# Attention and a capacity-limited mixture of experts on Trainium2: counting keys over fixed levels instead of a stepwise search, with the value logits split over four tiles and constants loaded later

## The chip, the cores and the metric

The kernel runs on one core of one Trainium2 chip. The metric is the device time of one execution in microseconds (us); a profiled execution also gives a span, from its first to its last instruction, which is a little shorter. TensorE (PE) does the matmuls, VectorE (DVE), ScalarE (ACT) and GpSimd (POOL) the element-wise work, and SyncE (SP) issues most of the transfers. Each engine works through its own instructions in order and waits for the others by semaphores.

## What is computed

```python
# q, k, v: 8 batches x 8 heads x 576 rows x 64, cut into chunks of 64 rows
scores = scale * q_c @ k_c^T                  # within a chunk, scale = 1/8
attn = exp(scores - max); attn /= attn.sum(-1) + 1e-9
x = (attn @ v_c), rows of all heads side by side     # N = 4608 rows x D = 512

logits = x @ w_gate                           # 8 experts
expert_idx = argmax(logits, axis=1)
gate_w = softmax(logits)[expert_idx]
for e in range(8):
    tok_idx = rows with expert_idx == e
    keep the `capacity` (80) of them with the greatest gate_w
    out[tok_idx] = gate_w * (relu(x[tok_idx] @ w1[e]) @ w2[e])     # F = 1024
# all other rows of out are zero
```

Everything is float32. The gate weight of a row's own expert is called its key; the kernel looks for a threshold per expert that about 80 keys pass, and then ranks the few rows that are left.

## The kernel before

The 4608 rows are 36 tiles of 128 (RT). Tiles 0 to 31 hold the first 512 rows of each of 8 batches, four tiles a group; tiles 32 to 35 hold the last 64 rows of every batch. The order of the work is written out by hand: one loop over i (L838 to L881) runs a pipeline over the tiles, and every engine gets its instructions in the order of that code.

Iteration i does the scores of tile i (TensorE, s, L330), then their row maximum and subtraction on VectorE (mx L336, sm L339). If a group of four is complete, it does its gate matmul (L464) and a copy (L470). Then come the transposes of sm of tile i-1 (pt, L360) with ScalarE's exponential that empties them (pT, L362), the values of tile i-2 (o, L387 or L377) with VectorE's division (rc L397 and L398, x L415), the transposes of x of tile i-3 (px, L351) with ScalarE's copy (xT, L458), and at its end the loads of qk and v some tiles ahead (NB = 8 and NV = 7 buffers). pt and px take turns in one PSUM bank (tag "tp"), so each waits until ScalarE has emptied the other. Weights of the first experts and the clearing of the output are issued at iterations that the tables EARLY and CLEAR name.

Small steps on VectorE ride in the gaps: `fill()` (L286) is called five times a tile and takes one step from the queue of bounds, one from the queue of gates, and one more from that of bounds. A step may also issue a ScalarE or a TensorE instruction, which then stands in that engine's order at this place.

The keys of the first 16 tiles (NS) give an interval that holds each expert's threshold. `search_keys` (L585) transposes them to kT, and three rounds narrow it by four each: `search_count` (ScalarE signs sg L625 with an accumulator, VectorE hits L629), `search_sum` (L632, one matmul) and `search_move` (L637, some VectorE steps, the last of which, nt and th, are read by the next round's signs). `bounds` (L677) makes an interval of 254 levels per expert. For each tile, `levels` (L542) turns the keys into a level number bo, and 256 signs (ScalarE `signs` L557) or steps (GpSimd `steps_` L562) of it are counted by `tally` (L567): matmuls with `mine`, the rows' expert as one of eight columns, and 256 levels as two halves of 128, plus a row of ones for tiles that hold signs; `left_add` (L697) subtracts each group's counts on VectorE. LEVELS says behind which tile each step of this is queued.

The tiles 32 to 35 get their gate logits another way: the values' own logits (v times w_gate, head by head) stand in the last 8 of 73 columns of vh, the values of those tiles. `value_logits` (L442) makes them in iteration 30, as 64 matmul calls (two instructions each) in one piece, from vT, which is loaded in two halves into buffers of qk; ScalarE copies them (L452).

Behind the loop stand the last tile's work, the tallies of tiles 28 to 35, `threshold` (L715), a mask, ranks, and the row numbers of each expert's kept rows; matmuls without use (`keep_warm`, L751) fill TensorE's pauses there. Then `experts` gathers the rows from the scratch copy xs (L179), and runs both layers (L204, L237) for six groups of 128 slots.

Of the kernel before, what the change touches and what calls it, by code (L numbers as in the profile page):

```python
# [8 lines left out]
F32 = mybir.dt.float32  # L9
BF16 = mybir.dt.bfloat16  # L10
# [11 lines left out]
NB = 8  # L22
NV = 7
# [8 lines left out]
NBP = NS // 2 * 8  # L32
NIT = 3
# [4 lines left out]
LEVELS = {15: "l0:4 c0 c1 c2 - - - - s2 c3", 19: "l4:5 - s3 s0 c4", 23: "l5:6 s4 s1 c5",  # L38
          27: "l6:7 s5 c6 - - - - - s6"}
LV, LP = 7, 8  # L40
# [4 lines left out]
EARLY = {6: [0], 14: [1], 22: [2], 28: [3, 4], 29: [5], 30: [6], 31: [7]}  # L45
CLEAR = {32: [0], 33: [1], 34: [2, 3]}


C_ID, C_IO, C_TR, C_TAU, C_BLK = 0, 128, 384, 512, 640
C_A = C_BLK + NBP  # L50
# [5 lines left out]
C_J3 = C_J + 48  # L56
C_F3 = C_J3 + 3
C_D3 = C_F3 + 3
C_V3 = C_D3 + 3
NCONST = C_V3 + 3  # L60


@with_exitstack
def attention_moe(ctx: ExitStack, tc: tile.TileContext, qk, vv, v8, vt, wg, w1, w2, cap, cst, out):
# [23 lines left out]
    step = cp.tile([P, NE], F32, name="step")  # L88
    thr = cp.tile([P, NE], F32, name="thr")
    idp = cp.tile([P, P], BF16, name="idp")  # L90
    rst = cp.tile([P, NE, RT], BF16, name="rst")
    low = cp.tile([P, NE], F32, name="low")
    slot_oob = cp.tile([P, NR], F32, name="slot_oob")
    inw = cp.tile([P, NE], F32, name="inw")
    left = cp.tile([P, 2, NE], F32, name="left")
    lob = cp.tile([P, NE], F32, name="lob")
# [172 lines left out]
    with ExitStack() as actx:  # L269
# [3 lines left out]
        ps2 = actx.enter_context(tc.tile_pool(name="ps2", bufs=2, space=PSUM))  # L273
# [3 lines left out]
        S = {}  # L277
        gates, bounds_q = deque(), deque()

        def step_one(queue):  # L280
            if queue:
                fn, args = queue.popleft()
                fn(*args)

        def fill():

            step_one(bounds_q)
            step_one(gates)
            step_one(bounds_q)

        def flush(queue):
            while queue:
                step_one(queue)
# [7 lines left out]

        vh = wk.tile([P, 4, 8, VX], F32, name="vh", tag="vh", bufs=1)
# [52 lines left out]
        def probs(i):  # L355
# [7 lines left out]
            d['pT'] = pT  # L363

        def values(i, last=False):
# [26 lines left out]
            d['pov'] = po[:, :, 0:260].rearrange("p j (m x) -> p j m x", m=4)  # L392

# [48 lines left out]
        def value_logits():  # L442

            pv = ps2.tile([P, 4, 8, NE], F32, name="pv", tag="g")
            for r in range(4):
                for c in range(8):
                    for h in range(2):
                        o = 64 * h
                        nc.tensor.matmul(pv[o:o + 64, r, c, :],
# [768 lines left out]
```

## Time and profile before

| what | us |
|---|---|
| median of three runs (264.30, 264.91, 267.28) | 264.91 |
| the profiled execution's own time | 263.62 |
| its span | 261.8 |
| first expert layer starts | 160.42 |
| last expert layer ends | 254.81 |
| TensorE busy, of the span | 237.4 (91%) |
| VectorE, ScalarE, GpSimd busy | 130.5, 76.1, 53.2 |
| mean granted clock of TensorE | 0.962 |

A row of the timeline reads: start, duration, engine, line, operation, result <- operands, shape, count, and in brackets how long the engine had been idle and who released it. A row of the windows reads: the stretch and its length, then for each engine busy time and number of instructions, the granted clock, the mean share of the DMA engines and GB/s. A row of the groups reads: line, engine, operation, shape, count, busy us, mean ns of one, and the idle time just before them. A row of the waits reads: who waited for whom, us in all, times, the longest. TensorE's float32 matmuls are two instructions each; a loading of weights (PEld) stands beside the matmul it belongs to.

### The profile page before, as it was taken

What the parts mean: (1) busy time and instruction counts of PE and PEld (TensorE: products, weight loads), DVE (VectorE), ACT (ScalarE), POOL (GpSimd) and SP (SyncE); (2) the same over time, 40 slices, a digit from 0 to 9 for tenths busy, and PEclk for the clock granted to TensorE, in tenths of its full rate; (3) what the DMA queues carried; (4) which work ended last, traced back from release to release, by engine and by line L of the source; (5) the groups of instructions that cost most, each with busy time, mean ns of one, the idle gap of its engine ahead of it and who ended that gap; (6) DMA issues with size and microseconds to landing.
All of it is one profiled execution on the core that took longest, in us unless ns stands there. A gap on an engine that the chain in (4) does not pass through costs nothing. (4 is left out here: it accounts for less than half of the span.)

```text
span 261.8 us, 8338 instructions
## 1 busy us (share of the span) xinstructions
PE 237.4 (91%) x3584; PEld 141.4 (54%) x3584; DVE 130.5 (50%) x423; ACT 76.1 (29%) x157; POOL 53.2 (20%) x115
## 2 busy tenths in 40 slices
PE   8789999999998798899888898999999999999970
PEld 5677767676766666868756573342423324232310
DVE  6688696968797779325869854111211211121210
ACT  2125434344454436325744400120200102010000
POOL 6021030303030304920312836100000111010110
PEclk9999999999999999859999799999999999999995
DMA  7999999999999999999997305999999999995011
GB/s 246 304 358 368 406 397 404 353 374 390 408 356 409 413 412 377 348 412 400 405 401 301 100 0 155 382 387 408 396 401 408 402 398 395 405 386 196 3 38 36
DMA packets 32554, 86.01 MB, mean 328 GB/s; under 512 B 3264, under 2 KB 3392, under 8 KB 32384
## 3 DMA queue, kind: packets, MB, share of 16 engines
q1 hardware_dynamic: 28768, 72.50, 72.9%
q0 software_dynamic: 3456, 12.32, 12.5%
q10 hardware_dynamic: 288, 0.59, 0.9%
q8 instruction: 30, 0.49, 0.8%
q14 instruction: 12, 0.10, 0.1%
HBM read 65.22 MB, written 20.45 MB: 327 GB/s over the span
## 5 line engine op out<-in xcount | busy, mean ns | idle before, releaser
L204 PE MATMUL hc<-w,xtc 128*32 128x512 f32 x384 | 44.2, 594 | 0.2 <-ACT xtc L194 0.2
L237 PE MATMUL yc<-w,htc 128*32 128x512 f32 x384 | 43.3, 593 | 0.0
L387 PE MATMUL o<-vb,pT 128*64 128x130 f32 x512 | 36.2, 283 | 0.2 <-PE pt L360 0.2
L336 DVE TENSOR_REDUCE mx<-s 128x8 f32<-128x512 f32 x36 | 24.7, 685 | 15.7 <-PE s L330 15.2
L387 PEld LDWEIGHTS o<-vb,pT 128*64 128x64 f32 x512 | 28.4, 138 | 5.7 <-issue 5.1
L362 ACT ACTIVATE pT<-pt 128x512 f32<-128x512 f32 x36 | 21.5, 597 | 23.8 <-PE pt L360 23.4
L237 PEld LDWEIGHTS yc<-w,htc 128*32 128x32 f32 x384 | 12.5, 110 | 29.1 <-issue 28.2
L330 PE MATMUL s<-qk 64*64 64x64 f32 x1152 | 25.8, 227 | 2.3 <-issue 1.6
L360 PE MATMUL pt<-ct,sm 128*128 128x128 f32 x144 | 24.0, 290 | 3.8 <-ACT xT L458 2.7
L204 PEld LDWEIGHTS hc<-w,xtc 128*32 128x32 f32 x384 | 12.1, 110 | 26.0 <-issue 25.6
L339 DVE TENSOR_TENSOR sm<-s,mx 128x512 f32<-128x512 f32 x36 | 24.9, 691 | 0.7
L415 DVE TENSOR_TENSOR x<-o,rc 128x512 f32<-128x512 f32 x36 | 24.8, 689 | 0.5
L458 ACT COPY xT<-px 128x512 f32<-128x512 f32 x32 | 18.6, 580 | 19.6 <-PE px L351 19.4
L330 PEld LDWEIGHTS s<-qk 64*64 64x64 f32 x1152 | 20.9, 136 | 5.3 <-issue 2.6
L360 PEld LDWEIGHTS pt<-ct,sm 128*128 128x128 f32 x144 | 15.4, 143 | 14.6 <-issue 7.5
L243 POOL DMA_INDIRECT out<-ysc,si x6 | 6.0, 995 | 84.7 <-DMA out<-zero 42.3
L209 ACT ACTIVATE hsc<-hc 128x512 f32<-128x512 f32 x6 | 3.6, 598 | 64.3 <-PE hc L204 64.3
L428 POOL DMA_DIRECT2D xs<-x x8 | 6.6, 820 | 75.5 <-DVE keys L509 69.5
L242 DVE TENSOR_SCALAR ysc<-yc,gatec 128x512 f32<-128x512 f32 x6 | 4.5, 751 | 34.4 <-PE yc L237 34.4
L351 PE MATMUL px<-ct,x 64*128 64x64 f32 x256 | 14.8, 235 | 1.4 <-ACT pT L362 1.4
L211 DVE TENSOR_SCALAR hsc<-hc 128x512 f32<-128x512 f32 x6 | 4.1, 691 | 22.6 <-PE hc L204 22.6
L226 DVE COPY htc<-hpc 128x512 f32<-128x512 f32 x6 | 4.1, 692 | 22.0 <-PE hpc L222 22.0
(163 smaller groups left out, 264.3 us busy)
## 6 DMA issues: line engine op xcount, KB each, us to landing
w<-in_w SPq DMA_DIRECT2D x12, 2048.0 KB, 20.3
qk<-in_qk SPq DMA_DIRECT2D x35, 512.0 KB, 7.3
out<-zero SPq DMA_DIRECT2D x9, 1024.0 KB, 13.8
vb<-in_vv SPq DMA_DIRECT2D x64, 130.0 KB, 6.8
xs<-x POOLq DMA_DIRECT2D x8, 1024.0 KB, 9.9
w<-in_w SPq DMA_DIRECT2D x8, 1024.0 KB, 10.3
vh<-in_v SPq DMA_DIRECT2D x1, 1168.0 KB, 11.0
vT<-in_vt SPq DMA_DIRECT2D x2, 512.0 KB, 8.3
```

Of the source, the lines that this page charges most:

```text
L204: nc.tensor.matmul(h[o:o + 32, :], lhsT=xT[r][:, b, o:o + 32], rhs=getw(groups[r][g])[0][:, b, 512 * f:512 * f + 512], start=(b == 0), sto ...
L237: nc.tensor.matmul(y[o:o + 32, :], lhsT=hT[r][c // 4][:, c % 4, o:o + 32], rhs=getw(groups[r][g])[1][:, c, :], start=(c == 0), stop=(c == ...
L330: nc.tensor.matmul(ps[64 * u:64 * u + 64, h, 64 * pr:64 * pr + 64], lhsT=t['q'][64 * h:64 * h + 64, pr, u, :], rhs=t['k'][64 * h:64 * h + ...
L336: nc.vector.tensor_reduce(mx, s8, axis=AX.X, op=ALU.max)
L339: nc.vector.tensor_tensor(sm.rearrange("p c h k -> p h c k" if T == 8 else "p c k h -> p h c k"), s8, mx[:, :, :, None].to_broadcast([P, 2 ...
L351: nc.tensor.transpose(pm[:, u, 64 * pr:64 * pr + 64], src(pr)[rows], ident[rows, rows])
L360: nc.tensor.transpose(pt[:, pr, :], sv[:, pr, :], ident)
L362: nc.scalar.activation(pT, pt, AF.Exp, scale=0.125)
L387: nc.tensor.matmul(po[64 * u:64 * u + 64, pr // 2, o:o + 130].rearrange("p (h x) -> p h x", h=2), lhsT=d['pT'][:, pr, 64 * u:64 * u + 64], ...
L415: nc.vector.tensor_tensor(t['x'][:, r, :].rearrange("p (m j e) -> p j m e" if T == 8 else "p (j m e) -> p j m e", j=2, m=4), U[i]['pov'][. ...
L428: nc.gpsimd.dma_start(xs[T * 576:T * 576 + 512].rearrange("(c p) d -> p c d", p=P), t['x'])
L458: nc.scalar.copy(t['xT'][:, :, P * r:P * r + P].rearrange("p a (u j) -> p a u j", u=2), pm)
```

## The change

The search is replaced by counts over 128 fixed levels. For each of the first 16 tiles, `hist_sign` (ScalarE, L630 of the changed kernel) compares 128 fixed levels (and one that all pass) with the rows' keys, 128x129, and `hist_add` (TensorE, L638) adds them up by expert, in PSUM (tile ph, 8 rows x 129). `bounds` reads from the counts the interval for each expert on 8 partitions, with two VectorE instructions that multiply by the levels' distances and accumulate, and some small ones.

The counts of the levels are kept by expert too: `tally` is one matmul of 129 columns per tile into one PSUM tile pc, without `left_add`; there are 126 levels where 254 were, and signs are 128x129, steps 128x128. For this PSUM bank the pool ps2 has two tags with one buffer each in place of one tag with two.

ScalarE's small work (the exponentials of the gates and all signs) goes through two queues, `exps` and `signs_q`. An entry may be taken four fills after it was queued (LAG), by `act_slot`: at most two behind the exponential pT, at most one behind the copy xT. TensorE's counts go through a queue `counts`, at most four at an iteration's end (`pe_slot`), an iteration after their sign. `drain` empties all queues behind the loop.

`value_logits` does 16 calls (32 instructions) behind the values of each of the tiles 28 to 31, into free columns of their PSUM bank, and ScalarE copies them behind the next xT. vT has a buffer of its own, loaded at iteration 22, and vh is loaded at 25; NB is 7, NV 6. Three loads of constants move behind the loads of tile 5, and a fourth (hc, the fixed levels) is new; `late_constants` comes one iteration later. EARLY and CLEAR change a little.

On TensorE, before, where the value logits stand as one piece (tile 30's scores are behind, s_2295 is tile 31's):

```order
L351 MATMUL px_2218<-ct,x_1872 128x64 x8
L449 MATMUL pv<-wgp,vT_1751 64x8 x32
L449 MATMUL pv<-wgp,vT_1752 64x8 x32
L330 MATMUL s_2295<-qk_1840 64x64 x16
L464 MATMUL L_2320<-xT_1873,wgp 32x512 x4
L360 MATMUL pt_2327<-ct,sm_2170 128x128 x4
L387 MATMUL o_2334<-vb_105,pT_2177 64x130 x8
```

The changed kernel at the same place, from the scores of tile 30 to those of tile 31:

```order
L356 MATMUL s_2137<-qk_1827 64x64 x16
L386 MATMUL pt_2168<-ct,sm_2089 128x128 x4
L414 MATMUL o_2181<-vb_111,pT_2096 64x130 x8
L476 MATMUL o_2181<-wgp,vT 64x8 x16
L377 MATMUL px_2212<-ct,x_1871 128x64 x8
L624 LDWEIGHTS mine
L624 MATMUL pc<-lv_2099,mine 8x129
L624 LDWEIGHTS mine
L624 MATMUL pc<-lv_2128,mine 8x129
L356 MATMUL s_2230<-qk_1902 64x64 x16
```

A quarter of the value logits now stands between the values and px, and three more such pieces follow in the next iterations; the counts by expert (pc) stand at the iteration's end.

On ScalarE, before, at the first round of the search, between two exponentials pT:

```order
L592 COPY kT<-pk 64x256
L362 ACTIVATE pT_1558<-pt_1553 128x512
L625 ACTIVATE sg_0_1577,cn_1576<-kT,nt 64x256
L625 ACTIVATE sg_1_1579,cn_1576<-kT,nt 64x256
L458 COPY xT_1284<-px_1584 128x4x128
L470 COPY lt_1625<-L_1620 128x512
L362 ACTIVATE pT_1632<-pt_1627 128x512
```

ScalarE in the changed kernel, at the first group's signs (hv, of tiles 0 to 3, in iterations 11 and 12):

```order
L490 COPY xT_499<-px_777 128x4x128
L630 ACTIVATE hv_787<-hc,gg_590 128x129
L504 COPY lt_819<-L_814 128x512
L388 ACTIVATE pT_826<-pt_821 128x512
L630 ACTIVATE hv_828<-hc,gg_590 128x129
L630 ACTIVATE hv_830<-hc,gg_590 128x129
L490 COPY xT_763<-px_858 128x4x128
L630 ACTIVATE hv_868<-hc,gg_590 128x129
L388 ACTIVATE pT_904<-pt_899 128x512
```

The signs stand in the same places, behind a pT or an xT, but they read constants and the keys (gg) of a group that was gated before, not a step of the same search; they stand in iterations 11 to 24, and there are sixteen of them where the search had six.

On VectorE, before, in the search's first move (jk, jx, lo and wd are its steps):

```order
L397 TENSOR_SCALAR rc_1643<-o_1634 128x8
L398 RECIPROCAL rc_1643<-rc_1643 128x8
L645 SCALAR_TENSOR_TENSOR jk_1648,n_1649<-pc_1645,cv 64x3
L650 SCALAR_TENSOR_TENSOR jx_1651,lo<-jk_1648,ct 64x3
L415 TENSOR_TENSOR x_1560<-o_1634,rc_1643 128x512
L650 SCALAR_TENSOR_TENSOR jx_1654,wd<-jk_1648,ct 64x3
L656 TENSOR_SCALAR lo<-lo 64x1
L336 TENSOR_REDUCE mx_1701<-s_1684 128x8
```

VectorE in the changed kernel, where the interval is read from the counts ph:

```order
L362 TENSOR_REDUCE mx_1781<-s_1764 128x8
L583 TENSOR_TENSOR mine<-wt_1679,mw_1682 128x32
L660 TENSOR_SCALAR c_1576<-ph,cap_100 8x1
L365 TENSOR_TENSOR sm_1785<-s_1764,mx_1781 128x2x256
L662 TENSOR_SCALAR c_1576<-ph 8x1
L664 SCALAR_TENSOR_TENSOR n_1577,lo_101<-ph,c_1576,hc 8x128
L426 TENSOR_SCALAR rc_1806<-o_1797 128x8
L667 SCALAR_TENSOR_TENSOR n_1577,hi_102<-ph,c_1576,hc 8x128
```

What were many steps over 64 partitions is now two instructions over the 128 levels and a few small ones, once.

The diff, cut to its core:

```diff
-NB = 8
-NV = 7
+NB = 7
+NV = 6
...
-LEVELS = {15: "l0:4 c0 c1 c2 - - - - s2 c3", 19: "l4:5 - s3 s0 c4", 23: "l5:6 s4 s1 c5",
...
+LAG = 4
...
-        ps2 = actx.enter_context(tc.tile_pool(name="ps2", bufs=2, space=PSUM))
+        ps2 = actx.enter_context(tc.tile_pool(name="ps2", bufs=1, space=PSUM))
...
+        def act_slot(most):
+
+            for _ in range(most):
+                ready = [q for q in (exps, signs_q) if q and S['t'] - q[0][0] >= LAG]
+                if ready:
+                    ready[0].popleft()[1]()
+
+        def pe_slot(most=4):
+
+            for _ in range(most):
+                if not counts or counts[0][0] > S['i']:
+                    return
+                counts.popleft()[1]()
...
             nc.scalar.activation(pT, pt, AF.Exp, scale=0.125)
             d['pT'] = pT
+            act_slot(2)
...
             d['pov'] = po[:, :, 0:260].rearrange("p j (m x) -> p j m x", m=4)
+            if i >= 28:
+                value_logits(i - 28, po[:, 0, 320:384].rearrange("p (c e) -> p c e", c=8))
...
-            pv = ps2.tile([P, 4, 8, NE], F32, name="pv", tag="g")
-            for r in range(4):
-                for c in range(8):
-                    for h in range(2):
...
+            for c in range(8):
+                for h in range(2):
+                    o = 64 * h
+                    nc.tensor.matmul(pv[o:o + 64, c, :], lhsT=S['vT'][o:o + 64, r, c, :],
+                                     rhs=wgp[o:o + 64, c // 2, 0:NE], start=True, stop=True)
+            S['pv'] = r, pv
...
-            lv = gk.tile([P, 2 * P], BF16, name=f"lv{rt}", tag="lv", bufs=LV)
-            nc.scalar.activation(lv, io_b, AF.Sign, bias=bo[:, rt:rt + 1], scale=-1.0)
-            U[rt].update(lv=lv, signs=True)
+            lv = gk.tile([P, P + 1], BF16, name=f"lv{rt}", tag="lv", bufs=LV)
+            nc.scalar.activation(lv, io_l, AF.Sign, bias=bo[:, rt:rt + 1], scale=-1.0)
+            U[rt]['lv'] = lv
...
+            nc.tensor.matmul(S['pc'][:, 0:lv.shape[1]], lhsT=mine[:, rt, :], rhs=lv,
+                             start=S['cnt'] == 0, stop=last)
...
+        def hist_sign(r0, rt):
+            hv = gk.tile([P, P + 1], BF16, name=f"hv{rt}", tag="lv", bufs=LV)
+            nc.scalar.activation(hv, hc[:, H_T:H_T + P + 1], AF.Sign,
+                                 bias=U[r0]['g'][:, rt - r0:rt - r0 + 1], scale=-1.0)
+            counts.append((S['i'] + 1, lambda: hist_add(rt, hv)))
...
+            nc.tensor.matmul(S['ph'], lhsT=mine[:, rt, :], rhs=hv,
+                             start=S['hist'] == 1, stop=S['hist'] == NS)
...
-            nc.sync.dma_start(ct[:, C_ID + P:], cst[:, C_ID + P:])
-            nc.sync.dma_start(wgp[:, :, 0:8], wg.rearrange("(b p) e -> p b e", p=P))
-            nc.sync.dma_start(capi, cap[0:1, :].broadcast_to([P, 2]))
             for n in range(4, NB):
                 load_qk(n)
                 if n < NV:
                     load_v(n)
+                if n == 5:
+                    nc.sync.dma_start(ct[:, C_ID + P:], cst[:, C_ID + P:])
+                    nc.sync.dma_start(wgp[:, :, 0:8], wg.rearrange("(b p) e -> p b e", p=P))
+                    nc.sync.dma_start(capi, cap[0:1, :].broadcast_to([P, 2]))
+            nc.sync.dma_start(hc, hst)
...
-                if i == 30:
-                    value_logits()
-                if i == 24:
-                    S['vT'] = [wk.tile([P, 2, 8, 64], F32, name=f"vT{j}", tag="qk", bufs=NB)
-                               for j in range(2)]
-                    for j in range(2):
-                        nc.sync.dma_start(S['vT'][j], vt[j])
+                pe_slot()
+                if i == 22:
+                    nc.sync.dma_start(S['vT'], vt)
+                if i == 25:
                     nc.sync.dma_start(vh, v8)
```

More of the change, by code (lines that the diff above doesn't have):

```diff
@@ L31 @@
 NS = 16
-NBP = NS // 2 * 8
-NIT = 3
+NL = 126
 NWARM = 25
@@ L513, in key @@
                     parts()
+                if rt < NS:
+                    for j in range(rt, rt + n):
+                        signs_q.append((S['t'], lambda j=j: hist_sign(rt, j)))
             def parts():
@@ L564, in steps_ @@
-            eng.tensor_scalar(lv, io_b, bo[:, rt:rt + 1], 2.0, op0=ALU.is_le, op1=ALU.mult)
-            U[rt].update(lv=lv, signs=False)
-        def tally(rt, n):
-            ph = ps2.tile([P, 2, NE], F32, name=f"ph{rt}", tag="g")
-            rts = range(rt, rt + n)
-            ab = [j for j in rts if U[j]['signs']]
-            for b in range(2):
-                for j in ab:
-                    nc.tensor.matmul(ph[:, b, :], lhsT=ones_b, rhs=mine[:, j, :],
-                                     start=j == ab[0], stop=False)
-                for j in rts:
-                    nc.tensor.matmul(
-                        ph[:, b, :], lhsT=U[j]['lv'][:, P * b:P * b + P], rhs=mine[:, j, :],
-                        start=not ab and j == rt, stop=j == rt + n - 1)
-            U[rt]['ph'] = ph
@@ new lines, in steps_, with tally @@
+            eng.tensor_scalar(lv, io_b[:, 0:P], bo[:, rt:rt + 1], 2.0, op0=ALU.is_le, op1=ALU.mult)
+            U[rt]['lv'] = lv
+        def tally(rt, last=False):
+            if S['cnt'] == 0:
+                S['pc'] = ps2.tile([NE, P + 1], F32, name="pc", tag="acc")
+            lv = U[rt]['lv']
+            assert S['cnt'] or lv.shape[1] > P
+            nc.tensor.matmul(S['pc'][:, 0:lv.shape[1]], lhsT=mine[:, rt, :], rhs=lv,
+                             start=S['cnt'] == 0, stop=last)
+            S['cnt'] += 1
@@ L914, in attention_moe @@
             for w in "ab":
-                flush(tails[w])
-            for rt in (28, 32):
-                count(rt, "v")
+                while tails[w]:
+                    step_one(tails[w])
+            count(32)
             late = S.pop('late')
@@ L923, in attention_moe @@
             nc.scalar.copy(io_h, io_b[:, P:2 * P, None].to_broadcast([P, P, HOT]))
-            left_add(28, 4)
-            tally(32, 4)
+            for j in range(28, RT):
+                tally(j, j == RT - 1)
             keep_warm(1)
```

351 lines of the change are left out of this document (161 added, 190 removed).

## The prediction

> **What bounds the kernel now.** I read the page's first two parts, then the windows by stage, then the timeline of TensorE and ScalarE inside the two stages that are longer than their neighbours. The page first:
>
> ```profile
> span 261.8 us, 8338 instructions
> PE 237.4 (91%) x3584; PEld 141.4 (54%) x3584; DVE 130.5 (50%) x423; ACT 76.1 (29%) x157; POOL 53.2 (20%) x115
> PEclk9999999999999999859999799999999999999995
> DMA  7999999999999999999997305999999999995011
> ```
>
> TensorE is busy 91% of the span, but that is an average over two halves, and the clock row has a dip at its 17th and 18th slice, a shorter one at the 23rd. I cut the span where VectorE starts the row maximum (mx, L336) of tiles 8, 20, 28, 32 and 35, and where the first expert layer starts and ends.
>
> ```profile
> core 0: us, PE busy (x) PEld busy (x) DVE busy (x) ACT busy (x) POOL busy (x), PEclk, DMA share, GB/s
> 30.05:68.19 38.14, 37.35 (x757) 27.71 (x757) 30.53 (x91) 16.33 (x30) 6.89 (x24) 1.00 1.01 387
> 68.19:97.46 29.27, 25.95 (x515) 19.33 (x515) 23.61 (x94) 14.15 (x33) 4.60 (x16) 1.00 1.03 398
> 97.46:121.70 24.24, 22.03 (x421) 17.55 (x421) 12.18 (x47) 9.46 (x21) 11.27 (x16) 0.79 1.00 383
> 121.70:132.06 10.36, 9.37 (x239) 7.71 (x240) 9.12 (x37) 8.07 (x18) 2.29 (x8) 1.00 1.05 402
> 132.06:160.42 28.36, 23.34 (x325) 17.67 (x323) 20.82 (x98) 8.06 (x22) 12.26 (x24) 0.94 0.50 180
> 160.42:254.81 94.39, 93.03 (x836) 31.60 (x836) 13.22 (x21) 10.02 (x18) 8.79 (x10) 1.00 0.86 327
> ```
>
> The first row is the undisturbed loop: 12 tiles in 38.14 us, TensorE busy 37.35 of them. It is the bound, at 12.71 us for four tiles. At that rate the eight tiles of the second row (20 to 27) need 25.43 us and take 29.27, a loss of **3.84**. The four tiles of the third row need 12.71 and take 24.24: **11.53** lost, at a mean clock of 0.79. The three of the fourth need 9.53 and take 10.36. The last row, the experts, is TensorE again (93.03 of 94.39), and the change does not touch it, so what the attention gains reaches the end if the stage between passes it on.
>
> Where the second row loses it, in two neighbouring iterations:
>
> ```profile
> 82.87 0.51 ACT L625 ACTIVATE sg<-kT,nt 64x256 bf16<-64x256 f32 x1 [1.24 <-DVE nt L663]
> 83.29 0.19 ACT L625 ACTIVATION_READ_ACCUMULATOR sg<-kT,nt 64x1 f32 x1
> 83.38 0.49 ACT L625 ACTIVATE sg<-kT,nt 64x256 bf16<-64x256 f32 x1
> 84.50 0.46 PE L351 MATMUL px<-ct,x 64*128 64x64 f32 x8 [1.12 <-ACT pT L362]
> 88.25 0.51 ACT L625 ACTIVATE sg<-kT,nt 64x256 bf16<-64x256 f32 x1 [1.25 <-DVE nt L663]
> 89.86 0.66 PE L360 MATMUL pt<-ct,sm 128*128 128x128 f32 x4 [1.51 <-ACT xT L458]
> ```
>
> A sign of the search (L625) stands at the head of ScalarE's queue and waits 1.24 us for VectorE's next step; the exponential (pT) or the copy (xT) that TensorE needs is queued behind it, and TensorE then stands 1.12 and 1.51 us. These two are 2.63 of the 3.84.
>
> Where the third row loses it:
>
> ```profile
> 106.58 1.79 PE L449 MATMUL pv<-wgp,vT 64*64 64x8 f32 x54
> 109.31 3.91 PE L449 MATMUL pv<-wgp,vT 64*64 64x8 f32 x70 [0.94 <-issue]
> 114.52 0.69 DVE L336 TENSOR_REDUCE mx<-s 128x8 f32<-128x512 f32 x1 [7.16 <-PE s L330]
> 105.29:108.70 3.41, 3.08 (x88) 1.00 0.95 317
> 108.70:118.94 10.24, 9.63 (x134) 0.50 1.03 413
> ```
>
> The 128 matmuls of the value logits (pv) run as one block from 106.58 to 113.22, so VectorE waits 7.16 us for the scores of tile 31; and from 108.70 to 118.94 the granted clock is 0.50. The last two rows are windows of TensorE alone, with busy time, clock and DMA share. 54 of the matmuls took 33 ns each before the drop, 70 took 56 ns each after it.
>
> **The change part by part.**
>
> *Value logits.* The 128 matmuls stay, but as 32 behind each of the values of tiles 28 to 31, that is in iterations 30 to 33, two of which lie before mx of tile 32. At 33 ns, 32 cost 1.06 us, all on TensorE. The block is gone, and with it the half-speed stretch if it came from the block. The tallies (ph) go as well, and counts by expert come, six of 129 columns. Their price is not in the trace. The nearest row is this:
>
> ```profile
> 138.38 3.45 PE L751 MATMUL pwarm<-io_b,ones_b 128*128 128x256 bf16 x30
> 124.33 0.26 PE L574 MATMUL ph<-mine,ones_b 128*128 128x8 bf16 x4
> 124.44 0.24 PE L577 MATMUL ph<-mine,lv 128*128 128x8 bf16 x4
> 124.54 0.24 PE L574 MATMUL ph<-mine,ones_b 128*128 128x8 bf16 x4
> 121.70:132.06 10.36, 1.08 (x24) 0.88 (x24) 1.00 1.05 402
> 121.70:132.06 10.36, 0.91 (x16) 0.67 (x16) 1.00 1.05 402
> ```
>
> 256 columns come every 115 ns (3.45 / 30), 8 columns every 26 ns (four in the 0.105 us between starts); the last two rows count the tallies from tile 32 to 35, 24 and 16 matmuls of L577 and L574. 129 columns lie between; I take half of 115, 58 ns. So tiles 28 to 31 should take 12.71 + 2 × 1.06 + 6 × 0.058 = 15.18 where they took 24.24: **−9.06**. The bounds: 12.71 + 2.12 + 6 × 0.026 at the least, and 5.1 us more if the clock halves again (a rival).
>
> *Tiles 32 to 34.* Two more pieces of value logits come in (+2.12), 40 tally matmuls at 26 ns go (−1.05), eight counts come (+0.46): **+1.5**. The other counts of the loop stand behind the last tile, where the 30 warm-up matmuls above only pass time; they cost nothing there, and 0.8 us (14 × 58 ns) if that cover were gone.
>
> *Search out, counts over levels in.* Transposes, three rounds of signs, hits and sums go; no ScalarE instruction of the new count reads something that VectorE has yet to make, since each sign is taken from its queue only four fills after its key was issued. So the 3.84 go: **−3.84**. In their place 16 ScalarE signs of 128x129 come in iterations 11 to 24, 16 counts on TensorE, and some 15 small VectorE instructions once. The counts: 16 × 58 ns = **+0.9** (0.4 to 1.8). The signs: the nearest rows are 128 columns in 0.391 and 256 in 0.499.
>
> ```profile
> L739 ACT ACTIVATE ab<-io_b,ptok 128x128 bf16<-128x128 bf16 x3 | 1.2, 391 | 0.0
> L559 ACT ACTIVATE lv<-io_b,bo 128x256 bf16<-128x256 bf16 x25 | 11.2, 499 | 3.8 <-DVE bo L554 3.8
> 30.80 0.60 ACT L362 ACTIVATE pT<-pt 128x512 f32<-128x512 f32 x1 [0.81 <-PE pt L360]
> 34.98 0.59 ACT L458 COPY xT<-px 128x512 f32<-128x512 f32 x1 [0.78 <-PE px L351]
> ```
>
> ScalarE is idle 0.81 us before each pT and 0.78 before each xT. At most two signs stand behind a pT, at most one behind an xT. Back to back, a ScalarE instruction starts 0.09 us before the one ahead ends (82.87 + 0.51 against 83.29, above); two of 0.391 then fill 0.69 of the gap. I cost them at nothing; the cover is that idle time, and it is only 0.1 wide for pairs.
>
> *Bounds of the levels on VectorE.* VectorE is busy 30.53 of 38.14 us in the loop. Two instructions read 8x128 counts with an accumulator; the nearest are
>
> ```profile
> L975 DVE SCALAR_TENSOR_TENSOR bt<-kr,kc,ct 128x128 bf16<-128x128 f32 x8 | 2.7, 346 | 1.0 <-PE kr L992 1.0
> L975 DVE DVE_READ_ACCUMULATOR bt<-kr,kc,ct 128x1 f32 x8 | 0.7, 83 | 0.0
> L689 DVE TENSOR_SCALAR step<-hib 128x8 f32<-128x8 f32 x1 | 0.2, 160 | 0.0
> ```
>
> so 0.43 each. At least nothing (VectorE's idle fifth takes them), at most the whole 3.84 back. I take **+0.8**, both of them exposed once, since one stands behind a sm and the other between rc and its reciprocal in the order, ahead of the x that px waits for; the 13 others are single ones of 0.16 in many fills, as the search's were.
>
> *Constants later.* One wait for a load of qk is in the trace:
>
> ```profile
> PE s L330 <- DMA qk<-in_qk: 0.6, 1, 0.6
> PEld yc L237 <- DMA w<-in_w: 0.9, 1, 0.9
> ```
>
> Moving three loads behind those of tile 5 can save 0 to 0.6; **−0.3**. One buffer less for qk and for v costs nothing while the loads lead by more than one tile's 3.2 us: the one wait above says that they do.
>
> *Tail.* The threshold gains one VectorE instruction and the reading of an accumulator (0.16 + 0.08) and a transpose, and loses one update of left; four 128x128 steps stand for three 128x256 and a sign. **+0.2** (−0.3 to +0.5).
>
> Sum: −9.06 + 1.5 − 3.84 + 0.9 + 0.8 − 0.3 + 0.2 = **−9.8**. The profiled execution took 263.62, which makes 253.8. The median of the three runs shown is 264.91, 1.29 above it; I put that on top: **255.1 us**.
>
> **The rivals.**
>
> *A. The clock halves again.* Before the drop TensorE was not idle: 3.08 of 3.41 us busy (the window row above), 0.94 us of waiting behind it. It was busy with matmuls of 8 columns. The new kernel still issues 128 of them, in four pieces. If these small matmuls are what lowers the clock, a stretch like 108.70:118.94 comes back: 10.24 us at half speed do 5.1 us of work, so 255.1 + 5.1 = 260.2. Against it: each piece of 1.06 us now stands among the 3.2 us of a tile's other work (12.71 / 4). [...] 0.12.
>
> *B. The transfers keep the gain.* The DMA share is 1.00 to 1.05 from tile 8 to tile 35: 63.87 us from tile 20 to 35 become about 54, and the bytes stay. What did not fit slides behind tile 35, where the share is 0.50 of 28.36, so 14 us are free against 10 that slide. The first gather must find the last rows written:
>
> ```profile
> 144.87 1.26 POOL L423 DMA_DIRECT2D xs<-x  x2 [2.22 <-DVE left L702]
> 155.91 1.18 POOL L179 DMA_INDIRECT xgc<-xs,gic  x1 [3.94 <-DVE bt L975]
> ```
>
> It would come at about 146. If those writes or the second expert's weights land behind the backlog, some 3 to 4 us are lost: 258 to 259. Against it: loads waited for cost 0.6 and 0.9 us in all so far. 0.08.
>
> *C. Slower: the signs stand in TensorE's way.* ScalarE gets 36 signs up to the last tile's gating, 16 of them new (the level signs, 25 of 0.499 now, become narrower). If a 128x129 sign takes more than about 0.45, a pair outgrows the 0.8 us gap and the xT or pT behind it is late, as the waits of 1.12 and 1.51 show. From there the price is the signs themselves, at worst all of them: 36 × 0.39 = 14.1, and 269.2 us. For it speaks only that the gap is narrow; against it, that 16 come over 14 iterations and the rest over eight. 0.04.
>
> *D. The change does not do what it says.* The levels or the queue hold TensorE up as the search did, in another form, and only the value logits gain: 255.1 + 3.84 = 259.0. 0.04.
>
> **How the numbers follow.** The forecast has 0.72. Its own range is the sum's: counts (0.5 and 0.45), bounds (0.8), constants (0.3) and tail (0.5) at their low ends give 2.55 less, and the offset to the median is 0.68 with the lowest run (264.30), so 251.9; at the high ends of the counts, constants and tail it is 2.3 more, with the bounds 5.3. B, D and half of A lie up to 260. So 251.5 to 260.0, the last 0.4 below for a part of the 0.83 us that tiles 32 to 34 lose now. One per cent, 2.65 us, is about what a measurement tells from no change. Below 262.3 lie the forecast nearly whole, A, B and D: 0.91 faster. Within 1%: 0.06, a late piece of several together or A with B. Slower: 0.03, C at its worst.
>
> **What would show it.** Right: no clock below 1.00 between tiles 28 and 35 in the windows; four pieces of 32 value-logit matmuls of about 1.06 us; mx of tile 28 to that of 32 in about 15.2 us; tiles 20 to 28 in about 26 to 27; no wait of pt or px for ScalarE above 0.5 us; the first gather near 146; the experts again 94 us. Wrong: a half-speed stretch that begins in iterations 30 to 33 (A); TensorE or the gather waiting for a load (B); ScalarE's gap before pT gone where pairs of signs stand (C); tiles 8 to 20, which get the first signs, above 38.14 by more than the 0.5 that their nine counts cost.

## The result and the profile after

Four runs of the changed kernel take 255.07 us in the median (253.29 to 258.40), four of the kernel before 264.61 us (261.96 to 267.28): a ratio of 0.9649, 95% interval 0.9537 to 0.9761. The ratio leaves out the longest run of each kernel (258.40 and 267.28), which is over 1.5% above its shortest; the medians count it. The profiled execution takes 254.82 us with a span of 253.0, against 263.62 and 261.8: 8.8 us less, where the sum said 9.8.

The windows of the changed kernel by the same stages: mx of tiles 8, 20, 28, 32 and 35, and the first and last expert layer.

```profile
core 0: us, PE busy (x) PEld busy (x) DVE busy (x) ACT busy (x) POOL busy (x), PEclk, DMA share, GB/s
29.23:67.67 38.44, 38.05 (x766) 28.37 (x767) 30.38 (x90) 19.78 (x42) 7.00 (x24) 1.00 1.03 400
67.67:93.44 25.77, 25.35 (x514) 18.94 (x514) 22.34 (x80) 12.16 (x25) 5.66 (x18) 1.00 1.03 397
93.44:108.52 15.08, 15.02 (x323) 11.69 (x324) 10.77 (x35) 8.35 (x21) 6.81 (x15) 1.00 1.04 405
108.52:121.66 13.14, 10.94 (x269) 8.90 (x270) 8.55 (x30) 6.22 (x17) 2.35 (x8) 0.98 1.03 401
121.66:150.06 28.40, 25.07 (x304) 18.54 (x304) 20.98 (x98) 8.38 (x24) 12.08 (x24) 0.89 0.80 306
150.06:244.58 94.52, 93.08 (x836) 31.51 (x836) 12.44 (x20) 10.01 (x18) 8.51 (x9) 1.00 0.86 326
```

One row of before has to be put right for the comparison. The stretch to 254.81 ended 1.36 us behind the last matmul; the experts of before took this:

```profile
160.42:253.45 93.03, 93.03 (x836) 31.60 (x836) 12.47 (x20) 10.02 (x18) 8.53 (x9) 1.00 0.87 332
```

| stage | before | after | difference | forecast |
|---|---|---|---|---|
| start to tile 8 | 30.05 | 29.23 | -0.82 | -0.3 |
| tiles 8 to 19 | 38.14 | 38.44 | +0.30 | +0.5 |
| tiles 20 to 27 | 29.27 | 25.77 | -3.50 | -2.6 |
| tiles 28 to 31 | 24.24 | 15.08 | -9.16 | -9.06 |
| tiles 32 to 34 | 10.36 | 13.14 | +2.78 | +1.5 |
| tile 35 to the experts | 28.36 | 28.40 | +0.04 | +0.2 |
| experts | 93.03 | 94.52 | +1.49 | 0 |
| behind the last matmul | 8.4 | 8.4 | 0 | 0 |

The stage with the largest term comes out within 0.1 us of its forecast. That alone does not show that it falls for the reason forecast; the experiments ask that first. The timeline of TensorE in the changed kernel first, with the counts by expert, two of the four pieces of value logits, and the only wait of TensorE above 0.2 us in the stages of tiles 28 to 34:

```profile
98.21 0.22 PE L624 MATMUL pc<-lv,mine 128*8 128x129 bf16 x1
100.61 1.10 PE L476 MATMUL o<-wgp,vT 64*64 64x8 f32 x32
102.03 0.28 PE L624 MATMUL pc<-lv,mine 128*8 128x129 bf16 x2
107.50 0.33 PE L624 MATMUL pc<-lv,mine 128*8 128x129 bf16 x3
113.95 1.32 PE L476 MATMUL o<-wgp,vT 64*64 64x8 f32 x32
121.25 0.37 PE L356 MATMUL s<-qk 64*64 64x64 f32 x2 [2.08 <-issue]
```

Each count adds 0.055 us (0.22, 0.28, 0.33 for one, two, three), three of the four pieces take 1.10 and the last 1.32, where 0.058 and 1.06 were priced. New is the 2.08 us in the middle of tile 35's scores, in which TensorE waits for nothing that the profile shows ("issue"); the kernel before had 0.94 of the same kind inside its block. The clock falls for one stretch right behind it, told by the windows of TensorE alone (busy, clock, DMA share, GB/s):

```profile
117.76:121.18 3.42, 1.34 (x44) 1.00 1.05 387
121.18:124.59 3.41, 3.33 (x42) 0.50 1.04 417
```

### The profile page after: what moved, and what is told of

Same layout as the page of the kernel before. It is cut to its first block, busy times and chain, and to the rows that moved or that the text cites. A ratio compares the mean times of both kernels' runs of the same rounds, so it can differ in the third digit from the quotient of the medians.

```text
span 253.0 us, 8153 instructions
## 1 busy us (share of the span) xinstructions
PE 233.5 (92%) x3505; PEld 137.8 (54%) x3505; DVE 126.4 (50%) x393; ACT 75.1 (30%) x163; POOL 50.0 (20%) x117
## 4 chain that ended last, share of the span: by engine, by line
PE 69%; DMA 14%; DVE 6%; ACT 4%; issue 3%; POOL 1%; POOLq 0%; DVEq 0%; ACTq 0%
PE yc L228 14%; PE hc L195 13%; PE o L414 12%; DMA w<-in_w 9%; PE pt L386 8%; PE px L377 5%; PE s L356 5%; ACT xT L490 4%; PE L L498 3%; DMA xs<-x 2%; PE pw L789 2%; PE hpc L213 2%; DMA vb<-in_vv 2%; PE o L476 2%; PE lT L510 2%
## 5 line engine op out<-in xcount | busy, mean ns | idle before, releaser
L414 PE MATMUL o<-vb,pT 128*64 128x130 f32 x512 | 35.4, 279 | 0.1
L414 PEld LDWEIGHTS o<-vb,pT 128*64 128x64 f32 x512 | 27.6, 135 | 5.5 <-issue 4.3
```

Of the source, the lines that this page charges most:

```text
L414: nc.tensor.matmul(po[64 * u:64 * u + 64, pr // 2, o:o + 130].rearrange("p (h x) -> p h x", h=2), lhsT=d['pT'][:, pr, 64 * u:64 * u + 64], ...
```

## The experiments

Times of stages are from each run's own profile, one for each run, between the starts of the same mx. They are steadier than whole executions: where a run leaves them alone, tiles 20 to 27 take 25.76 or 25.77 us (the changed kernel and runs 1, 5, 6, 10, 11 and 12) and tiles 28 to 31 15.08 to 15.10 (the changed kernel and runs 6, 8, 11 and 12). Tiles 32 to 34 take 12.88 to 13.53 in the latter five, and the way from tile 0 to tile 8 takes 22.43 to 23.59.

**1. The block put back into the changed kernel.**

```diff
-            if i >= 28:
-                value_logits(i - 28, po[:, 0, 320:384].rearrange("p (c e) -> p c e", c=8))
...
                 pe_slot()
+                if i == 30:
+                    pv = ps2.tile([P, 4, 8, NE], F32, name="pv", tag="g")
+                    for r in range(4):
+                        value_logits(r, pv[:, r])
+                    S.pop('pv')
+                    nc.scalar.copy(vh[:, :, :, 65:VX], pv)
```

> The changed kernel with the value logits put back as one piece of 128 matmuls at the end of iteration 30 (copied at once by ScalarE), all else as changed. Theory (the piece and the half clock behind it are the 9.1 us of tiles 28 to 31): mx of tile 28 to mx of tile 32 takes 24 us (23.4 to 24.8) with a stretch of clock 0.50 in it, tiles 32 to 35 give 2.1 us back, and the median is about 261.5. Rival (the half clock had another cause than these matmuls): the stage takes 12.7 + 0.35 + 128 x 0.033 + 0.9 = 18.2 us at clock 1.00, and the median is about 256.

Measured: 256.81 us in the median (0.9694 of before, interval 0.9581 to 0.9807). The windows of its two stages:

```profile
94.70:114.71 20.01, 19.86 (x387) 15.54 (x388) 10.91 (x35) 8.52 (x20) 6.85 (x15) 0.83 1.01 386
114.71:123.99 9.28, 8.61 (x205) 6.71 (x206) 8.57 (x30) 5.72 (x14) 2.35 (x8) 1.00 1.03 399
```

And its TensorE around the fall of the clock:

```profile
101.32:104.73 3.41, 3.41 (x98) 1.00 0.91 308
104.73:111.56 6.83, 6.83 (x106) 0.50 1.02 391
```

Both theories miss. The half clock comes back with the block, so it does belong to these matmuls; but the stage takes 20.0 us, not 24, and 3.86 of the 4.93 that it loses come back in the next stage (9.28 against 13.14). Splitting the block is worth 1.07 us in tiles 28 to 34 of the two profiles (29.29 against 28.22; 0.7 to 1.3 against runs 6, 8, 11 and 12, with 27.98 to 28.63), and 1.7 in medians of different sessions, which is not clear of the spread. These tiles gained 6.38 in all (34.60 to 28.22), so most of it has another source.

**2. Only the split, in the kernel before.**

```diff
             d['pov'] = po[:, :, 0:260].rearrange("p j (m x) -> p j m x", m=4)
+            if i >= 28:
+                value_logits(i - 28, po[:, 0, 320:384].rearrange("p (c e) -> p c e", c=8))
...
-                if i == 30:
-                    value_logits()
```

> The kernel before with only the value logits split: 32 matmuls behind the values of tiles 28 to 31; search, tallies, buffers and loads as before. Theory (the two gains are separate): tiles 20 to 27 keep 29.3 us, tiles 28 to 31 take 12.71 + 2.12 + 40 x 0.026 = 15.9, tiles 32 to 34 take 10.36 + 2.12 = 12.5, the experts no more than 0.5 us longer than 93.0, median 264.6 - 8.3 + 2.1 = 258.4 (257 to 260). Rival (the search's new form is what lets the value logits be hidden): tiles 28 to 31 stay above 18 us and the median above 261.

Measured: 267.54 us in the median of four that lie between 262.20 and 269.95, with the kernel before at 265.19 (262.07 to 268.34) beside it; whole executions do not tell the two apart. The profile is of the 262.20. The two stages, then TensorE at the fall of the clock:

```profile
97.34:114.46 17.12, 15.83 (x357) 12.42 (x357) 12.15 (x46) 9.29 (x22) 11.26 (x16) 1.00 1.02 387
114.46:131.09 16.63, 15.05 (x303) 12.83 (x304) 9.16 (x37) 8.48 (x21) 2.29 (x8) 0.69 1.04 403
```

```profile
115.74:119.16 3.42, 3.14 (x104) 1.00 1.02 408
119.16:129.40 10.24, 8.99 (x139) 0.50 1.05 403
```

The first stage falls to 17.12, 1.2 above the 15.9 expected, nearly all of it the three waits behind ScalarE that the kernel before has there too (0.26, 0.30 and 0.57); the second grows by 6.27. The half-clock stretch has not gone, it has moved, with its full 10.24 us, to the next iterations, where pieces of value logits and tallies stand together. That is the forecast's rival A, in the kernel before. Alone, the split gains 0.85 of the 6.38 (33.75 against 34.60 in the profiles), and nothing that the medians show. So the theory of two separate gains falls.

**3. and 4. Matmuls that compute nothing used, of 8 and of 64 columns.** Both add 64 matmuls behind the values of tile 8 and 128 behind those of tile 16, to the changed kernel. They differ in the number of columns and, with it, in the operand that is streamed and in where the unused sums land.

```diff
+            for _ in range({8: 2, 16: 4}.get(i, 0)):
+                t = TT[divmod(i + 2, 4)]
+                for c in range(8):
+                    for o in (0, 64):
+                        nc.tensor.matmul(po[o:o + 64, 0, 320 + 8 * c:328 + 8 * c],
+                                         lhsT=t['q'][o:o + 64, c // 2, c % 2, :],
+                                         rhs=wgp[o:o + 64, c // 2, 0:NE], start=True, stop=True)
...
+                                         rhs=t['k'][o:o + 64, c // 2, c % 2, :], start=True, stop=True)
```

> The changed kernel with matmuls of 8 columns added that compute nothing used (into free columns of PSUM): 64 behind the values of tile 8 and 128 behind those of tile 16, far from any fetch of value logits. Theory (matmuls of 8 columns in a row lower the granted clock when they fill a window of 3.4 us): the 64 (2.1 us) leave the clock at 1.00, the 128 (4.2 us) are followed by at least 3.4 us at 0.50; tiles 8 to 20 take 38.4 + 6.3 + 1.7 to 5. Rival (the clock fell since TensorE stood waiting for instructions): clock 1.00 unless TensorE stands 0.9 us or more there, tiles 8 to 20 take 38.4 + 6.3 = 44.7.

> The same as the run with matmuls of 8 columns, but with 64 columns each, the same number of instructions at the same places. Theory (few columns lower the clock): clock 1.00 throughout tiles 8 to 20. Rival (waiting for instructions does): the same half-clock stretch as with 8 columns, if TensorE stands as long there.

Measured, with 8 columns: tiles 8 to 20 take 51.61 us, above the 46.4 to 49.7 expected, with two stretches at half speed. TensorE in the windows of 3.41 us around the two insertions:

```profile
38.02:41.43 3.41, 2.79 (x98) 1.00 1.04 387
41.43:44.85 3.42, 3.42 (x19) 0.50 1.03 415
68.74:72.15 3.41, 3.14 (x108) 1.00 1.02 402
72.15:78.98 6.83, 5.33 (x64) 0.50 0.53 200
```

With 64 columns: 48.83 us, and at the same places

```profile
38.61:42.02 3.41, 2.80 (x80) 1.00 0.98 368
42.02:45.43 3.41, 3.41 (x57) 1.00 1.04 416
65.91:69.33 3.42, 3.31 (x108) 1.00 1.03 403
69.33:72.74 3.41, 1.73 (x58) 1.00 1.00 369
72.74:76.15 3.41, 3.41 (x37) 0.50 0.33 129
```

The pairs tell it apart. The windows at 38 us are equally busy (2.79 and 2.80 of 3.41): with 8 columns half speed follows, with 64 not. The windows of 108 matmuls at 68.74 and 65.91 are both nearly full: again only the 8 columns are followed by half speed. With 64 columns it falls one window later, behind 1.68 us in which TensorE stands without waiting for anything that the profile shows. So the clock was not 1.00 throughout, as the theory had it. Both few columns and standing came ahead of a lower clock here; busy time did not tell. Even 64 small matmuls (2.04 us of them) were enough, where the theory said that they are not.

**5. The pieces two iterations earlier.**

```diff
-            if i >= 28:
-                value_logits(i - 28, po[:, 0, 320:384].rearrange("p (c e) -> p c e", c=8))
+            if 26 <= i < 30:
+                value_logits(i - 26, po[:, 0, 320:384].rearrange("p (c e) -> p c e", c=8))
```

> The changed kernel with the four pieces of value logits behind the values of tiles 26 to 29 instead of 28 to 31. Theory (in iterations 33 to 35 so many small matmuls of tiles 32 to 34, value logits and counts come together that TensorE outruns its instructions, stands 2.08 us and then drops to half clock): with the pieces two iterations earlier the stand at tile 35's scores is below 0.7 us, no half-clock stretch lies between tile 28 and tile 35, the two stages take 12.71 + 4.4 + 0.33 = 17.4 and 9.53 + 0.46 = 10.0 us, 27.4 in sum against 28.2, and the median falls by 1 to 2 us to 253 to 254. [...]

Measured: 255.78 us in the median, against 255.07. Tiles 32 to 34 take 10.91, but tiles 28 to 31 19.92; the wait has moved into the last piece, and half speed follows it: the next four transposes take 1.11 us, which take 0.66 in run 1 at full clock (112.71):

```profile
108.58 0.98 PE L476 MATMUL o<-wgp,vT 64*64 64x8 f32 x28
110.80 0.38 PE L476 MATMUL o<-wgp,vT 64*64 64x8 f32 x4 [1.23 <-issue]
111.11 1.11 PE L510 MATMUL lT<-ct,lt 128*128 128x128 f32 x4
```

The theory that it belongs to iterations 33 to 35 falls: the wait stands at another place, and the two stages take 30.84 us, more than the 28.22 of the changed kernel.

**6. Three clearings moved ahead.**

```diff
-CLEAR = {33: [0], 34: [1, 2, 3]}
+CLEAR = {33: [0], 34: [1, 2, 3, 4, 5, 6]}
...
-                    for n in range(4, NT):
+                    for n in range(7, NT):
```

> The changed kernel with three of the five clearings of the output that are issued after the first expert group issued in iteration 34 instead (six there, none changed in size). Theory (the wait of 1.43 us for a weight at 213 us comes from the transfers, which fill the time from the first gather to there): that wait is gone, the experts take 93.1 us instead of 94.5, and the stage from tile 35 to the experts does not grow, since the transfers have 8 free us there; median 253.5 to 254.5. Rival (the three clearings only stand in the way earlier): the last rows of xs or the first weights land later, and the stage behind tile 35 grows by 1 us or more, median 255 to 257.

Measured: 261.62 us, 6.5 more than the changed kernel. The experts still take 94.47, and the stage ahead of them 35.08 instead of 28.40, since the first gathered rows come late:

```profile
PE xpc L183 <- DMA xgc<-xs,gic: 5.9, 1, 5.9
```

The rival is right, at a higher price than it named. The transfers idle for 5.7 us of this stage in the changed kernel (a share of 0.80 of 28.40), and that is no room for 3 MB more (an estimate: 7.5 us at the 401 GB/s of the stage ahead).

**7. No lag in ScalarE's queues.**

```diff
-LAG = 4
+LAG = 0
```

> The changed kernel with the lag of ScalarE's queues at 0 instead of 4 fills: a sign or an exponential may be taken at the next slot after it was queued, so it can stand at the head of ScalarE's queue before VectorE has made its operand. Theory (the lag is what keeps TensorE from waiting behind ScalarE): ScalarE waits 0.5 to 1.3 us for VectorE at each group's first sign and at its exponential, tiles 8 to 20 take 38.9 to 41 us instead of 38.4, tiles 20 to 28 26.3 to 27.5 instead of 25.8. Rival (any order without the search's chain of steps does, the lag is worth nothing): both stages within 0.3 us.

Measured: tiles 8 to 20 38.58 (38.44 with the lag), tiles 20 to 28 26.17 (25.77). The lag is worth 0.14 and 0.40 us; the rival holds for the first stage and nearly for the second. So it is not the lag that removes the search's 3.84; that its chain of steps was the cost, and not its place in ScalarE's order, is argued from this.

**8. Each sign of the fixed levels twice.**

```diff
+            h2 = gk.tile([P, P + 1], BF16, name=f"h2{rt}", tag="h2", bufs=1)
+            nc.scalar.activation(h2, hc[:, H_T:H_T + P + 1], AF.Sign,
+                                 bias=U[r0]['g'][:, rt - r0:rt - r0 + 1], scale=-1.0)
```

> The changed kernel with each of the 16 signs of the fixed levels done twice on ScalarE, the second into a tile that nothing reads. Theory (the idle 0.8 us of ScalarE covers a pair, not more): behind an xT two signs are still covered, behind a pT four of them take 0.39 + 3 x 0.30 = 1.3 us, 0.5 more than the gap, once a group; tiles 8 to 20 take 39 to 40 us instead of 38.4, tiles 20 to 28 26.0 to 26.6 instead of 25.8. Rival (TensorE has slack against ScalarE that the rows of before do not show): no change beyond 0.2 us.

Measured: 38.44 and 25.76, to 0.01 us what it was. ScalarE at the place with four signs behind a pT:

```profile
40.00 0.60 ACT L388 ACTIVATE pT<-pt 128x512 f32<-128x512 f32 x1
40.50 0.40 ACT L630 ACTIVATE hv<-hc,gg 128x129 bf16<-128x129 f32 x1
40.79 0.40 ACT L633 ACTIVATE h<-hc,gg 128x129 bf16<-128x129 f32 x1
41.08 0.39 ACT L630 ACTIVATE hv<-hc,gg 128x129 bf16<-128x129 f32 x1
41.38 0.39 ACT L633 ACTIVATE h<-hc,gg 128x129 bf16<-128x129 f32 x1
41.97 0.59 ACT L490 COPY xT<-px 128x512 f32<-128x512 f32 x1 [0.20 <-PE px L377]
```

The four end 0.2 us before the next xT could start. The signs stand in the iteration in which TensorE also does a group's gate matmul and the transposes of its logits, so that xT starts 1.97 us behind pT there (1.96 in the changed kernel, with two signs) and not 1.38 as in the plain iteration of before (33.60 and 34.98). The theory falls: the signs have room for as many again.

**9. The kernel before without its search.** It leaves out the three rounds, with empty steps in their place and a constant lower end of the interval.

```diff
-            for i in range(NIT):
-                for j in range(2):
-                    bounds_q.append((search_count, (i, j)))
-                bounds_q.extend([wait] * 7)
-                bounds_q.append((search_sum, (i,)))
-                search_move(i)
+            bounds_q.append((lambda: v.memset(lo, 0.125), ()))
+            bounds_q.extend([wait] * 50)
```

> The kernel before without the three rounds of its search: the interval starts at a constant 0.125 and its place in the queue is filled with as many empty steps; it leaves out signs, hits, sums and moves, and keeps levels, tallies, the value logits in one piece and all else. Theory (the rounds' waits at the head of ScalarE's queue are the loss in tiles 20 to 27, and what tiles 28 to 34 lose besides comes from the level signs, the tallies, the block and the clock): tiles 20 to 28 take 25.4 to 26.3 us instead of 29.3, tiles 28 to 35 keep 33.5 to 35.5. Rival (the search's delay is also what makes tiles 28 to 34 long): tiles 28 to 35 fall to 29 to 31, as in the changed kernel with the block put back.

Measured: 261.24 us, 0.9811 of before (0.9731 to 0.9891). Its windows of tiles 20, 28 and 32:

```profile
68.91:94.87 25.96, 25.43 (x509) 18.84 (x509) 21.05 (x69) 11.25 (x21) 4.61 (x16) 1.00 1.01 390
94.87:119.20 24.33, 22.03 (x421) 17.18 (x421) 12.27 (x46) 9.45 (x21) 11.29 (x16) 0.79 0.98 379
119.20:129.30 10.10, 9.22 (x239) 7.65 (x240) 9.03 (x36) 7.94 (x18) 2.30 (x8) 1.00 1.04 397
```

The theory holds for tiles 20 to 27: the search costs 3.31 us there. Behind them the time is the same as before (34.43 against 34.60), but it is made up in another way. TensorE waits for a load there, which the kernel before never does in these tiles:

```profile
101.89 0.88 PE L330 MATMUL s<-qk 64*64 64x64 f32 x32 [1.61 <-DMA qk<-in_qk]
```

The clock halves for 3.41 us behind this wait, and for 6.83 behind the block. In return the block has no wait of 0.94 in it, and a wait of 0.58 for xT is gone. So the run does not show that the search costs nothing in tiles 28 to 34. It shows that a shorter loop runs into its loads there; the changed kernel, which moves loads (vT has its own buffer, a weight load of iteration 22 comes later), has no such wait.

**10. Small matmuls behind each count.**

```diff
             S['cnt'] += 1
+            if S['i'] < RT - 1:
+                for _ in range(6):
+                    nc.tensor.matmul(S['po'][:, 0, 448:456], lhsT=lv[:, 0:P],
+                                     rhs=mine[:, rt, :], start=True, stop=True)
```

> The changed kernel with six matmuls of 8 columns added behind each count of the loop (84 from tile 28 to 35, the number of tallies that the kernel before has there; their sums go to unused columns). Theory (few columns in a row lower the clock, and the tallies were part of it): besides 84 x 0.026 = 2.2 us the clock falls to 0.50 for 3.4 to 10.2 us between tile 28 and tile 35, and the two stages take 31.5 to 35 us instead of 28.2. Rival (the tallies cost only their own time): 30.0 to 30.9 us, with at most the one half-clock stretch at the end that the changed kernel has.

Measured: 40.3 us in the two stages, more than the theory's 31.5 to 35, and 269.07 in the median. It does not tell what it was made for:

```profile
100.45 0.29 PE L630 MATMUL o<-mine,lv 128*128 128x8 bf16 x6 [0.69 <-DVE x L445]
105.70 0.29 PE L630 MATMUL o<-mine,lv 128*128 128x8 bf16 x6 [1.13 <-ACT vh L485]
112.43 0.29 PE L630 MATMUL o<-mine,lv 128*128 128x8 bf16 x6 [0.65 <-ACT vh L485]
```

The added matmuls write to a bank that VectorE and ScalarE still read, and wait for them, 5.4 us in six waits; the tallies of before had a bank of their own. The clock does fall, from 114.50 to 124.73 and from 128.15 to 131.56, but the waits have their part in it. What the tallies by themselves did to the clock stays open.

**11. Without the five clearings behind the first expert group.**

```diff
-                    for n in range(4, NT):
+                    for n in range(4, 4):
```

> The changed kernel without the five clearings of the output behind the first expert group: 5 MB that are not written (rows of the last five ninths that no expert keeps are left as they are). Theory (the experts' 94.5 us contain one wait for a weight since the transfers from the first gather on are behind): 93.0 to 93.2 us, no wait for a weight. Rival (the weight waits for a free buffer, not for bandwidth): 94.5 us still.

Measured: 252.06 us; rows of the last five ninths of the output that no expert keeps stay unwritten. The experts:

```profile
150.90:242.95 92.05, 92.04 (x836) 31.41 (x836) 12.44 (x20) 10.01 (x18) 8.47 (x9) 1.00 0.74 278
```

92.05 instead of 94.52, with no wait for a weight left: 2.47 us less, where 1.4 were expected, since the loading into TensorE (PEld) had waited 2.3. So the clearings hold the weight up, and not a free buffer. Whether it is their bytes, or their place ahead of the weight in SyncE's order, was not told apart.

**12. Constants ahead of tile 4's loads again.**

```diff
+            nc.sync.dma_start(ct[:, C_ID + P:], cst[:, C_ID + P:])
+            nc.sync.dma_start(wgp[:, :, 0:8], wg.rearrange("(b p) e -> p b e", p=P))
+            nc.sync.dma_start(capi, cap[0:1, :].broadcast_to([P, 2]))
             for n in range(4, NB):
...
-                if n == 5:
```

> The changed kernel with the three loads of constants back ahead of the loads of tile 4. Theory (moving them saves the one wait for qk): mx of tile 0 to mx of tile 8 takes 22.9 us, as before (30.05 - 7.19), instead of 22.6, and TensorE waits 0.3 to 0.6 us for a load of qk. Rival (the loads have enough lead either way): 22.6 us, no wait.

Measured: from mx of tile 0 to that of tile 8 22.79 us, against 22.61 changed and 22.86 before, with 0.4 us of waiting for a load of qk. The theory is not shown: runs 1, 7 and 8 load the constants as the changed kernel does and take 23.53, 23.59 and 23.52, with waits for a load of qk of 1.2, 1.1 and 0.8 us.

No run beats the changed kernel with the whole computation done, by more than runs differ.

## Why the prediction was right, and where it was not

*The size was right, the owner of the largest term was not.* "The block is gone, and with it the half-speed stretch" was to bring 9.06 us in tiles 28 to 31 and cost 1.5 behind them. The step that failed is taking the steady 12.71 (and two pieces and six counts) as what is left when the block is split: that credits the split with everything else that held these tiles up. By run 1 the split is worth 4.93 in the stage and loses 3.86 in the next; by run 2, alone in the kernel before, it is worth 0.85 in both together. That -9.16 came for -9.06 is luck. The rest of the 6.38 us that tiles 28 to 34 gained is between the kernel before and run 1, which both have the block: 34.60 against 29.29, 5.31 us. Three things differ there: the search (run 9 leaves its part open), the form and the order of the counts, and the moved loads. No run takes them one by one, but rows give the sizes. The kernel before waited four times for a pT or xT that stood behind ScalarE's small work, three times behind level signs and once, the first, behind a gate's exponential:

```profile
100.42 0.65 PE L360 MATMUL pt<-ct,sm 128*128 128x128 f32 x4 [0.27 <-ACT xT L458]
102.41 0.46 PE L351 MATMUL px<-ct,x 64*128 64x64 f32 x8 [0.30 <-ACT pT L362]
104.07 0.66 PE L360 MATMUL pt<-ct,sm 128*128 128x128 f32 x4 [0.58 <-ACT xT L458]
127.99 0.66 PE L360 MATMUL pt<-ct,sm 128*128 128x128 f32 x4 [0.36 <-ACT xT L458]
```

That is 1.51 us, and run 1 has none of it. The kernel before stood for 1.52 us without anything that the profile shows (0.94, 0.58), run 1 for 0.60; its half clock lasts 10.24, run 1's 6.83, which is 1.7 of work; 80 tallies of 26 ns against 14 counts of 55 are 1.3. Together 5.4, and the windows agree: of the 5.31, TensorE's busy time is 2.93 (31.40 to 28.47) and its idle time 2.38. This says where the time was, not which change removed it. The length of the half clock in particular is not settled: run 9 has the kernel before's block and tallies, and 6.83 us behind them.

*The tallies were under-priced.* "40 tally matmuls at 26 ns" is their own time only. Their counts rest on ScalarE's signs of 0.499 us, whose waits the forecast did not look for behind tile 28. In run 2 the half clock followed a stretch where tallies and value logits stand together; run 10 leaves open what the tallies do to it by themselves.

*Tiles 32 to 34*, +2.78 for +1.5: the 2.08 us in which TensorE stands were not in the sum, though the block's 0.94 of the same kind was in a quoted row. The last section lists such waits.

*The search*, -3.84: run 9 measures 3.31 for it. Of the 0.8 us for the bounds on VectorE, 0.25 came, at another place: a gate matmul (L498) waits that long for lbi (L679), a step of the bounds that reads pb, since pb and the gate's logits take turns in one PSUM buffer. All in all 25.77 is no more than the steady 25.43 and seven counts (0.39).

*The signs*: nothing, as forecast, though the reason was too narrow. The gap was taken from plain iterations, and run 8 shows that they fall into longer ones. Rival C had no ground to stand on.

*The constants*, -0.3: not shown. The start is 0.82 shorter, and the 0.25 of it that fall behind mx of tile 0 are less than the same start differs between runs (22.43 in run 6, 23.59 in run 7). The other 0.57 have nothing to do with the change: the 25 warm-up matmuls, before and after, are

```profile
1.05 5.45 PE L804 MATMUL pw<-warm 128*128 128x256 bf16 x25 [1.05 <-DVE warm L796]
```

```profile
1.05 4.88 PE L789 MATMUL pw<-warm 128*128 128x256 bf16 x25 [1.05 <-DVE warm L781]
```

since after the change they come every 0.21 us only up to 5.1 us, and every 0.11 us from there; before, all 25 come every 0.21 us, the last at 6.1 us.

*Rival B came true in part, at another place.* The gather found its rows; but the experts waited for a weight, before and after:

```profile
PEld yc L237 <- DMA w<-in_w: 0.9, 1, 0.9
```

```profile
PEld yc L228 <- DMA w<-in_w: 2.3, 1, 2.3
```

1.4 us more, nearly all of the 1.49 that the experts lost, which the forecast had at nothing.

*Rival A* did not come in the changed kernel, and came in run 2, as long as priced (10.24 us). The changed kernel's one half-clock stretch ahead of the tail follows a window in which TensorE mostly stands (1.34 of 3.42 us busy), and it costs little: runs 7 and 8 have the same wait (2.0 and 2.1 us) and no such stretch (a mean clock of 0.986 and 0.984, against 0.976), and their stage from tile 35 up to the experts takes 28.19 and 27.76 us, against 28.40.

*Two errors cancel in the time.* The sum is 1.0 us too large (9.8 for 8.8), and the 1.29 that was put on top for the median is 0.25 in the runs of the changed kernel. 255.1 for 255.07 is closer than its steps are.

## What to carry to other kernels

Before a stage's excess is given to its most visible instruction, put that instruction alone into the other kernel: here the split without the rest gained 0.85 us of 6.38. A price per matmul was not enough for the small ones: behind the 2.04 us of 64 of them in run 3 TensorE ran at half clock for 3.42 us. Leaving a part out can also bring a new wait: run 9 took the search out and met its loads (1.61 us), so that an equal time did not mean an equal stage. And when the first stage of a kernel with full transfers gets shorter, look for the load that the last stage will wait for (2.3 us here, 0.9 before).

## What the runs showed of the hardware

While matmuls ran, the clock was halved in these traces for 3.41 us or for two or three times that: 10.24 us from 108.70 in the kernel before, 6.83 from 104.73 in run 1, 3.41 from 121.18 in the changed kernel. The busy time of the 3.41 us ahead did not tell it: 3.08 us in the kernel before, 1.34 in the changed kernel, 3.14 in run 2, and all of it in runs 1 and 9. In run 9 the block of value logits, 8 columns each, runs from 106.55 without any pause (114 of them by 110.20):

```profile
106.30:109.71 3.41, 3.41 (x116) 1.00 0.86 287
109.71:116.54 6.83, 6.83 (x86) 0.50 1.02 403
```

In runs 3 and 4 windows as busy as each other (2.79 and 2.80 us; 3.14 and 3.31) were followed by half speed with 8 columns and by full speed with 64. The windows of 1.34 us in the changed kernel and of 1.73 in run 4 hold no matmul of 8 columns (64x8), and half speed came behind them too. How many columns or how much standing it takes, the runs do not say: runs 7 and 8 stand for 2.0 and 2.1 us at the same place as the changed kernel, with no half clock behind.

At some places TensorE stands without waiting for anything that the profile shows: in the changed kernel for 2.08 us in tile 35's scores (121.25), in the kernel before for 0.94 (109.31), 0.58 (129.88) and 1.06 us (136.47). In run 1 it is 0.60 us in tile 35's scores (123.68), in run 2 1.53 (120.41), in run 4 1.68 (72.51), in run 5 1.23 (110.80). Counted from TensorE's first instruction, with matmuls, loadings of weights and those of its sequencer, the 2.08 us of the changed kernel and the 0.58 us of the kernel before both end at number 4802, the one among scores, the other among values. What TensorE waits for there, and what sets how long, no run shows; that its instructions come late is a supposition in the expectations of runs 3 to 5.
